# Reordered instruction sequences, a new order of the input loads, and filler matmuls in the head of a fused attention and gated-mixer kernel

## The chip, the cores and the metric

The kernel runs on one core of one Trainium2 chip. The metric is the device time of one execution in microseconds (us); several executions of each kernel are timed and the median is given. A profile of one execution shows every instruction of the engines: TensorE (PE: matmuls, PEld: its weight loads), VectorE (DVE), ScalarE (ACT), GpSimd (POOL) and SyncE (SP, which only issues transfers).

## The reference

One sequence of 2048 tokens with 448 features passes two residual blocks, all in bfloat16:

```python
# A: attention over a dilated local window of 8 positions, step 2, 16 heads of 28
qkv = layernorm(x) @ wqkv                       # 448 -> 3 x 448
logits = q[s] . k[s - 2*w] * 28**-0.5           # w = 0..7; positions before the start are masked
h = x + (softmax(logits) @ v[s - 2*w]) @ wo
# B: gated mixing over all tokens
z = gelu(layernorm(h) @ w_in)                   # 448 -> 1792
z1, z2 = z[..., :896], layernorm(z[..., 896:])
g = w_sp @ z2 + b_sp[:, None]                   # 2048 x 2048 over tokens
out = h + (z1 * g) @ w_out                      # 896 -> 448
```

## The kernel before, in words

Tokens lie in 16 blocks of 128. Unit u holds the blocks u and u+8, one in each half of the partitions (64 features of each, seven slices `c`), so that two matmuls of 64 rows run side by side. All of the work is cut into named tasks. Each engine runs its tasks strictly in the order that a table of names, `ORDER`, gives it; semaphore waits follow from reads and writes of buffers. A planner (`Planner.run`) walks the five lists together with assumed durations and transfer rates (`bw=`), and so settles which of the eight PSUM banks a task gets (`acq`, `rel`); most tasks take a pair of banks. The rates change no transfer, only this walk. `eng.alts` tasks run on the engine in whose list they stand: a PSUM copy `ev...` can be in ACT's list or in VectorE's.

The tasks, in the order of the data:

- `x0` to `x15`, `xhalo`, `wqk0`, `wqk1`, `wv0`, `wv1`: loads, issued by SP and ACT (line 577 and after). `c_...`: constants, among them `c_dup` on POOL, a matrix that doubles rows.
- `bn1_b` (two instructions, lines 683 and 684), `rs1_u` (the inverse root: on ACT for unit 0, on POOL otherwise), `nrm1_b` (line 699): LayerNorm of block b. `bnh`, `rsh`, `nrmh`, `tTh`, `evh`: the same for the 16 tokens before the second half.
- `tT1_u` (line 714) and `ev1_u`: transposes of unit u on TensorE and their copy to SBUF, for units 0 to 2. `tD1_u`, `tD2_u` (line 706): transposes by DMA for all others and for the second LayerNorm.
- `dpq`, `dpk` (line 778): the query and key weights are spread over the partitions by a matmul with `dup`; `rpq`, `rpk` (line 664) copy the result back, two slices each, padded from 28 to 32 columns a head.
- `mmq`, `mmk` (line 821), `mmv` (861): projections, the first two in three ranges of columns (128; 384 or 398; 512). `evq`, `evk`, `evv`: their copies.
- For each of nine tiles i of 114 tokens: `mml` (896, logits, four groups of 16 matmuls), `exp` (909), `mask` (916), `mmr` (925, row sums), `ln`, `rex` (the inverse of the sums), `mmo` (945, four groups of 16), `ot` (963).
- For each unit: `mmy` (999, output projection), `h`, a second LayerNorm `bn2`, `rs2`, `nrm2`, then `mmz2` (1019) and its gelu `ge` (for units 0 to 2 first a raw copy `zr`), `bn3`, `ag3`, `rs3`, `nrm3`.
- `mmz1` (1082) with gelu `gz1`; then the mixing `g` (1120, 448 matmuls of 512 columns), `ua`, `um`, the last projection `wo` (1153), `oa` and the store `st`.
- `wsp`, `bb`, `w_out`, `win`: the later weights; the `wsp` transposes are paced by waits on steps such as `ge4_1` (lines 1175 to 1190).

Before any data is there, `warm` (line 658) runs eleven matmuls on a constant tile. `tab` marks a load of ACT's function table for the first half; exp and gelu need different tables.

Of the kernel before, what the change touches and what calls it, by code (L numbers as in the profile page):

```python
# [40 lines left out]
        xhalo x1 x0 x11 x9 x2 wqk1 x3 x10 x14 x15 x6 x7 wv0 x12 x4 x13 tD1_3 x5 tD1_4 tD1_7 tD1_6 tD1_5 tD2_1 tD2_0  # L41
        wsp0_0 wsp0_8 tD2_3 tD2_2 tD2_4 wsp0_1 tD2_5 wsp0_2 wsp0_9 tD2_7 tD2_6 wsp0_10 bb wsp0_3 w_out wsp0_4 wsp0_11
        wsp1_8 wsp0_5 wsp1_0 wsp0_12 wsp1_9 wsp0_6 wsp0_13 wsp1_1 wsp0_7 wsp0_14 wsp1_2 wsp0_15 wsp1_3 wsp1_10 wsp1_4
        wsp1_11 wsp1_5 wsp1_12 wsp1_13 wsp1_14 wsp1_6 wsp1_15 wsp1_7 st7 st4 st5 st3 st8 st6 st0 st10 st9 st14 st13
        st2 st12 st12b st1 st15 st11
""",
    "pool": """
        c_mband c_V c_nhalf c_ident c_ones c_dup c_kpad rs1_3 rs1_1 rs1_2 rs1_4 rs1_7 rs1_6 rs1_5 c_wo0 rs2_0 rs2_1
        rs2_2 rs2_3 rs2_4 rs2_5 rs2_7 rs2_6 rs3_0 rs3_4 rs3_5 rs3_1 rs3_3 rs3_2 rs3_6 rs3_7
""",  # L50
    "dve": """
        c_warm c_wqp bnh c_eps c_wkp c_xpad bn1_8 bn1_1 nrmh bn1_0 evh bn1_11 nrm1_0 bn1_3 nrm1_8 bn1_9 bn1_2 nrm1_3
# [48 lines left out]
TU = 8.706  # L101
NE = 2
# [285 lines left out]
def bass_sequential_preLN__sliding_local_dilated__mixer_gmlp__prompt_kernel(  # L388
# [18 lines left out]
    with contextlib.ExitStack() as top:  # L407
# [826 lines left out]
```

## Time and profile before

| what | us |
|---|---|
| median of 4 runs | 256.08 |
| lowest and highest | 255.47 and 256.32 |
| profiled execution, its own time | 255.47 |
| its span, first to last instruction | 253.7 |
| PE, DVE, ACT busy | 243.9, 141.9, 93.4 |
| PE waits by the view of waits, all of them | 6.5 |
| first transpose `tT1_0`; first projection | 11.48; 13.42 |
| first mixing matmul `g` | 132.8 |

Times within the profile count from the start of the span. In a timeline row stand the start, the duration of the merged group, engine, line, operation, tiles and count; an idle stretch before it and what ended it stand in brackets. A row of the chain has start, duration, engine, output and line. A row of the waits has who waited, for whom, the total, how often, and the longest. The name `reg` in a row stands for several tiles that share a buffer.

### The profile page before, as it was taken

How to read it: one execution, taken by the hardware profiler on the slowest of the kernel's cores; microseconds unless marked ns; L12 is line 12 of the kernel's file. 1: busy time of each engine (PE TensorE's matmuls, PEld its weight loads, DVE VectorE, ACT ScalarE, POOL GpSimd, SP SyncE). 2: the span in 40 equal slices, each digit the busy share in tenths (PEclk: the TensorE clock that was granted, in tenths of full speed). 3: DMA queues.
4: the chain of work that ended last, by engine and by line, in shares of the span. 5: the costliest groups of instructions: out<-in, count | busy, mean ns of one | idle time of the engine just before them, and what ended most of it. 6: DMA issues, size and time to landing. Idle time of an engine off the chain costs nothing.

```text
span 253.7 us, 6518 instructions
## 1 busy us (share of the span) xinstructions
PE 243.9 (96%) x2924; PEld 123.8 (49%) x2924; DVE 141.9 (56%) x280; ACT 93.4 (37%) x109; POOL 28.9 (11%) x72
## 2 busy tenths in 40 slices
PE   6499999999999999999999999999999999999995
PEld 2285544546657545444444444444444444444453
DVE  6797547678688888995972003145107051370653
ACT  2688837257756785787485000000000000000000
POOL 6133300000202120311450000000000000000000
PEclk9889999999999999999999999999999999999999
DMA  6953403252063688799699992030000000010222
GB/s 223 264 96 68 89 16 75 50 129 58 6 96 64 118 149 144 155 179 236 115 193 156 184 185 40 3 83 0 0 3 0 0 18 18 3 36 0 72 71 78
DMA packets 55556, 22.03 MB, mean 87 GB/s; under 512 B 46936, under 2 KB 55400, under 8 KB 55528
## 3 DMA queue, kind: packets, MB, share of 16 engines
q1 hardware_dynamic: 52096, 16.79, 34.3%
q10 hardware_dynamic: 3432, 4.82, 8.0%
q8 instruction: 23, 0.38, 0.6%
q14 instruction: 5, 0.04, 0.1%
HBM read 8.39 MB, written 1.84 MB: 40 GB/s over the span
## 4 chain that ended last, share of the span: by engine, by line
PE 89%; DVE 3%; ACT 3%; DMA 2%; SPq 1%; issue 0%
PE psum L1120 38%; PE psum L821 10%; PE psum L1153 8%; PE psum L1019 8%; PE psum L1082 8%; PE psum L999 5%; PE psum L861 4%; PE psum L896 3%; PE psum L945 2%; DMA x_tm<-in_A_x_dram 2%; ACT reg L909 1%; DVE reg L916 1%; ACT xh L664 1%; DVE reg L963 1%; PE psum L925 1%; SPq L577 1%
## 5 line engine op out<-in xcount | busy, mean ns | idle before, releaser
L1130 DVE TENSOR_TENSOR ub<-psum,reg 128x512 bf16<-128x512 f32 x28 | 18.9, 686 | 67.4 <-PE psum L1120 67.2
L1120 PE MATMUL psum<-reg,z2p 128*128 128x512 bf16 x224 | 49.5, 379 | 0.0
L1120 PE MATMUL psum<-wspT_lo,z2p 128*128 128x512 bf16 x224 | 48.7, 379 | 0.0
L1120 PEld LDWEIGHTS psum<-wspT_lo,z2p 128*128 128x128 bf16 x224 | 21.8, 98 | 26.6 <-DVE z2p L1066 0.4
L1120 PEld LDWEIGHTS psum<-reg,z2p 128*128 128x128 bf16 x224 | 21.9, 98 | 26.2
L821 PE MATMUL psum<-xh,reg 64*128 64x128 bf16 (+3 forms) x336 | 27.4, 313 | 0.5 <-ACT xh L664 0.3
L1019 PE MATMUL psum<-w_in,xh 64*128 64x448 bf16 x224 | 22.9, 349 | 0.0
L664 ACT ACTIVATE reg<-psum 128x896 bf16<-128x896 f32 (+5 forms) x26 | 20.5, 829 | 4.6 <-PE psum L778 2.8
L1153 PE MATMUL psum<-reg 128*128 128x448 bf16 (+1 forms) x119 | 22.2, 341 | 0.0
L909 ACT ACTIVATE reg<-psum 128x928 bf16<-128x928 f32 x18 | 16.9, 943 | 14.3 <-PE psum L821 8.7
L1082 PE MATMUL psum<-xh,w_in 64*128 64x512 bf16 x196 | 22.1, 376 | 0.0
L683 DVE BATCH_NORM_STATS2 st<-x_tm 128x6 f32<-128x448 bf16 x32 | 19.4, 605 | 2.2 <-DMA x_tm<-in_A_x_dram 2.2
L1050 DVE BATCH_NORM_STATS2 st<-z2p 128x6 f32<-128x448 bf16 x32 | 17.6, 608 | 3.0 <-ACT z2p L1044 3.0
L821 PEld LDWEIGHTS psum<-xh,reg 64*128 64x128 bf16 x336 | 13.7, 98 | 9.9 <-ACT xh L664 1.2
L669 POOL TENSOR_SCALAR rs<-mv 128x2 f32<-128x2 f32 x23 | 6.3, 272 | 99.0 <-DVE mv L684 80.9
L670 POOL TENSOR_TENSOR rs<-rs,nhalf 128x2 f32<-128x2 f32 x23 | 16.7, 728 | 1.9
L1153 PEld LDWEIGHTS psum<-reg 128*128 128x128 bf16 x119 | 11.6, 98 | 9.9
L1162 DVE TENSOR_TENSOR tring<-psum,x_tm 128x448 bf16<-128x448 f32 (+1 forms) x17 | 9.8, 591 | 11.9 <-PE psum L1153 11.8
L666 DVE CAST reg<-psum 128x1024 bf16<-128x1024 f32 (+3 forms) x11 | 12.3, 1122 | 6.6 <-PE psum L821 6.6
L1019 PEld LDWEIGHTS psum<-w_in,xh 64*128 64x128 bf16 x224 | 10.9, 94 | 9.8 <-issue 0.4
L1092 ACT ACTIVATE reg<-psum 128x1024 bf16<-128x1024 f32 x14 | 13.9, 1025 | 3.5 <-PE psum L1082 3.5
L1082 PEld LDWEIGHTS psum<-xh,w_in 64*128 64x128 bf16 x196 | 9.5, 94 | 11.3
(66 smaller groups left out, 222.0 us busy)
## 6 DMA issues: line engine op xcount, KB each, us to landing
w_in<-in_B_w_in_dram ACTq DMA_DIRECT2D x4, 448.0 KB, 4.9
x_tm<-in_A_x_dram SPq DMA_DIRECT2D x15, 112.0 KB, 5.0
out_dram<-tring SPq DMA_DIRECT2D x15, 112.0 KB, 1.7
w_in<-in_B_w_in_dram ACTq DMA_DIRECT2D x4, 336.0 KB, 4.3
reg<-in_B_w_out_dram SPq DMA_DIRECT2D x1, 784.0 KB, 6.3
z2p<-in_A_wqkv_dram ACTq DMA_DIRECT2D x1, 672.0 KB, 4.9
reg<-in_B_b_sp_dram SPq DMA_DIRECT2D x1, 512.0 KB, 5.2
reg<-in_A_wqkv_dram ACTq DMA_DIRECT2D x1, 392.0 KB, 6.3
```

The source lines that it names most:

```text
L664: iss("act", lambda e: e.activation(dst, src, AF.Copy), reads=rd, writes=wr, after=after)
L670: iss("pool", lambda e: e.tensor_tensor(dst, dst, nh, ALU.pow), reads=rr + [r_nhalf], writes=rr)
L683: iss("dve", lambda e: e.bn_stats(st[:, b, :], x_tm[:, b, :]), reads=[r_x[b]], writes=[rl[b]])
L821: iss("pe", lambda e, c=c, s=s, gi=gi, lhs=lhs: e.matmul(psum[:, bk[s] * 512 + cw * gi:bk[s] * 512 + cw * gi + cw], lhs, xh[64 * s:64 * s ...
L909: iss("act", lambda e: e.activation(E[:, es[0], 2 * n:2 * n + 2, :], pair_view(lb, 0, 8 * JW), AF.Exp, scale=SCALE), reads=[r_bank[lb[0]], ...
L1019: iss("pe", lambda e, c=c, s=s: e.matmul(psum[:, zb[s] * 512:zb[s] * 512 + D], xh[64 * s:64 * s + 64, c, XO + 128 * u:XO + 128 * u + 128], ...
L1050: iss("dve", lambda e, b=b: e.bn_stats(st3[:, b, k, :], z2p[:, b, D * k:D * k + D]), reads=[r_z2[b][k]], writes=[r_st3[b][k]])
L1082: iss("pe", lambda e, c=c, s=s: e.matmul(psum[:, bk[s] * 512:bk[s] * 512 + 512], w_in[64 * s:64 * s + 64, c, 128 * f:128 * f + 128], xh[64 ...
L1092: iss("act", lambda e: e.activation(z1p[f].rearrange("p (s t) -> p s t", s=2)[:, :, 512 * ch:512 * ch + 512], pair_view(bk, 0, 512), AF.Ge ...
L1120: iss("pe", lambda e, b=b: e.matmul(psum[:, gb[0] * 512:gb[0] * 512 + 512], z2p[:, b, 128 * f:128 * f + 128], src[:, b, 512 * (tc % 2):512 ...
L1130: iss("dve", lambda e: e.tensor_tensor(ub[:, us_[0], :], psum[:, gb[0] * 512:gb[0] * 512 + 512], bb[:, 512 * tc:512 * tc + 512], ALU.add), ...
L1153: iss("pe", lambda e, f=f: e.matmul(psum[:, wb[0] * 512:wb[0] * 512 + c1 - c0], z1p[f][:, 128 * m:128 * m + 128], w_out[:, f, c0:c1], star ...
```

## The change

All five lists of `ORDER` are new; each holds the same tasks as before, except that ten PSUM copies change between ACT's and VectorE's list. Among other things SP's list begins with x0, xhalo and x3; POOL makes `dup` first; `ev1_0` moves to VectorE; ACT's `tab` moves from its end to its start; `mmz2_0_0` stands earlier. A new function `fill` issues matmuls of 512 columns on the constant tile `warm` into the bank that a task is about to use, ahead of four tasks of TensorE, five in all (`FILL`). The planner's assumed rates and issue times of some loads are others, and so is the step that its walk gives to the loads `win0`. Lines after the change are higher by some ten: 778 becomes 788, 714 becomes 722, 821 becomes 832, 896 becomes 908, 1019 becomes 1031, 1082 becomes 1094, 1120 becomes 1132.

```diff
 ORDER = {
     "sp": """
-        xhalo x1 x0 x11 x9 x2 wqk1 x3 x10 x14 x15 x6 x7 wv0 x12 x4 x13 tD1_3 x5 tD1_4 tD1_7 tD1_6 tD1_5 tD2_1 tD2_0
-        wsp0_0 wsp0_8 tD2_3 tD2_2 tD2_4 wsp0_1 tD2_5 wsp0_2 wsp0_9 tD2_7 tD2_6 wsp0_10 bb wsp0_3 w_out wsp0_4 wsp0_11
-        wsp1_8 wsp0_5 wsp1_0 wsp0_12 wsp1_9 wsp0_6 wsp0_13 wsp1_1 wsp0_7 wsp0_14 wsp1_2 wsp0_15 wsp1_3 wsp1_10 wsp1_4
...
+        x0 xhalo x3 x11 x9 x1 wqk1 x2 x12 x14 x10 x15 x6 x5 wv0 x13 x4 tD1_3 x7 tD1_6 tD1_5 tD1_7 tD1_4 tD2_0 tD2_1
+        tD2_2 wsp0_0 tD2_3 tD2_4 wsp0_8 wsp0_1 wsp0_9 wsp0_2 tD2_6 wsp0_10 wsp0_3 tD2_7 wsp0_11 tD2_5 wsp0_4 wsp0_12
+        w_out bb wsp0_13 wsp1_8 wsp0_5 wsp0_14 wsp1_0 wsp0_6 wsp1_9 wsp0_15 wsp1_1 wsp1_10 wsp0_7 wsp1_2 wsp1_11
...
     "pool": """
-        c_mband c_V c_nhalf c_ident c_ones c_dup c_kpad rs1_3 rs1_1 rs1_2 rs1_4 rs1_7 rs1_6 rs1_5 c_wo0 rs2_0 rs2_1
...
+        c_dup c_ones c_ident c_nhalf c_kpad c_V c_mband rs1_3 rs1_1 rs1_2 rs1_6 rs1_5 rs1_7 c_wo0 rs1_4 rs2_0 rs2_1
...
     "dve": """
-        c_warm c_wqp bnh c_eps c_wkp c_xpad bn1_8 bn1_1 nrmh bn1_0 evh bn1_11 nrm1_0 bn1_3 nrm1_8 bn1_9 bn1_2 nrm1_3
-        bn1_10 nrm1_1 nrm1_11 nrm1_9 nrm1_2 nrm1_10 bn1_4 bn1_7 bn1_12 bn1_6 bn1_15 bn1_14 nrm1_4 nrm1_12 nrm1_7
-        bn1_13 nrm1_6 nrm1_15 mask0 bn1_5 nrm1_14 evq1_3 nrm1_5 nrm1_13 evk1_1 ot0 evv1 mask1 evq2_2 evk2_0 evq2_0
-        mask2 evv3 ot1 evv4 evq2_1 evq2_3 mask3 ot2 h0 bn2_0 h1 mask4 bn2_9 bn2_8 ot3 bn2_1 mask5 nrm2_1 ot4 nrm2_9
-        nrm2_0 nrm2_8 evv7 h2 mask6 h3 ot5 bn2_2 bn2_3 bn2_11 bn2_10 mask7 ot6 h4 nrm2_3 nrm2_11 bn2_12 mask8 nrm2_2
-        bn2_4 nrm2_10 h5 nrm2_4 ot7 nrm2_12 bn2_13 bn2_5 h6 ot8 nrm2_5 bn3_0_0 h7 nrm2_13 bn2_7 bn2_15 bn2_6 bn2_14
-        nrm2_7 nrm2_15 nrm2_6 bn3_0_1 nrm2_14 ag3_0 bn3_2_1 bn3_3_1 bn3_4_1 nrm3_0 bn3_4_0 nrm3_8 bn3_3_0 ag3_4
...
+        c_warm c_eps c_wkp c_xpad c_wqp bnh bn1_8 bn1_0 nrmh bn1_3 nrm1_0 bn1_11 bn1_9 nrm1_8 evh bn1_1 ev1_0 bn1_2
+        bn1_10 nrm1_3 nrm1_1 nrm1_11 nrm1_9 nrm1_2 nrm1_10 bn1_14 bn1_6 bn1_13 bn1_15 nrm1_6 nrm1_14 bn1_5 bn1_7 mask0
+        nrm1_5 nrm1_7 nrm1_13 bn1_12 bn1_4 nrm1_15 evk1_2 nrm1_4 nrm1_12 evk1_1 ot0 evv1 evv3 mask1 evq2_0 mask2
+        evk2_0 ot1 evq2_2 mask3 ot2 evk2_3 h0 bn2_0 bn2_8 h1 mask4 ot3 bn2_1 bn2_9 mask5 ot4 evv5 nrm2_0 nrm2_8 nrm2_1
+        h3 nrm2_9 mask6 h2 ot5 bn2_10 bn2_3 bn2_11 bn2_2 mask7 h4 nrm2_3 nrm2_2 nrm2_10 ot6 nrm2_11 bn2_4 mask8 bn2_12
+        ot7 h5 nrm2_4 nrm2_12 bn2_13 ot8 h6 bn2_6 bn2_14 h7 bn2_5 bn2_7 nrm2_6 nrm2_14 nrm2_5 zr2_1 bn2_15 bn3_0_0
+        nrm2_7 nrm2_13 nrm2_15 bn3_1_0 bn3_4_0 bn3_4_1 bn3_0_1 bn3_1_1 bn3_2_0 bn3_2_1 bn3_3_1 bn3_3_0 bn3_5_0 ag3_3
...
     "act": """
-        x8 wqk0 rsh wv1 rpq1 rs1_0 rpk2 rpq0 rpq2 rpq3 ev1_0 rpk3 rpk0 rpk1 evq0_2 evq0_0 evk0_2 evk0_0 ev1_2 ev1_1
-        exp0_0 evv0 evk1_0 exp0_1 evq1_2 evq1_0 evq1_1 evk1_3 ln0 rex0 wo2 evv2 evk1_2 exp1_0 exp1_1 evk2_3 exp2_0 ln1
-        win1_00 exp2_1 wo1 wo3 rex1 wo0 ln2 exp3_0 win1_04 exp3_1 rex2 evk2_2 win1_10 evk2_1 ln3 exp4_1 win1_14 exp4_0
-        rex3 evv6 ln4 exp5_0 exp5_1 rex4 ln5 rex5 evv5 exp6_0 exp6_1 ln6 exp7_0 rex6 exp7_1 evv8 exp8_0 win0_00 zr0_1
-        exp8_1 ln7 zr1_1 win0_04 zr0_0 rex7 ln8 zr1_0 win0_10 rex8 ge0_1 ge0_0 ge3_0 win0_14 zr2_1 zr2_0 ge2_1 ge4_1
-        ge4_0 ge3_1 gz1_0_6 ge2_0 gz1_0_4 ge1_1 gz1_0_0 gz1_0_5 ge5_1 gz1_0_3 ge1_0 ge7_1 ge7_0 gz1_1_5 ge5_0 gz1_1_6
-        ge6_0 ge6_1 gz1_1_1 gz1_1_0 gz1_0_1 gz1_1_2 gz1_1_3 tab gz1_0_2 gz1_1_4
+        x8 wqk0 tab rsh wv1 rs1_0 rpq0 rpq1 rpq3 rpq2 rpk0 rpk1 rpk3 rpk2 evq0_0 evq0_2 evk0_2 evk0_0 ev1_1 ev1_2
+        exp0_0 evv2 exp0_1 evv0 evk1_0 evq1_1 evq1_2 evq1_0 ln0 rex0 evq1_3 win1_00 evk1_3 exp1_0 wo2 exp1_1 wo3
+        evk2_1 exp2_0 exp2_1 ln1 wo0 ln2 rex1 win1_04 exp3_0 evk2_2 wo1 exp3_1 evq2_1 rex2 ln3 win1_10 evq2_3 rex3
+        exp4_0 exp4_1 evv4 exp5_0 ln4 exp5_1 rex4 evv6 win1_14 exp6_0 ln5 exp6_1 win0_00 rex5 ln6 rex6 exp7_0 zr0_0
+        exp7_1 win0_04 evv7 ln7 exp8_0 evv8 exp8_1 rex7 zr1_0 win0_10 ln8 rex8 zr0_1 zr2_0 ge0_1 ge2_0 win0_14 zr1_1
+        ge1_0 ge4_1 ge0_0 ge3_1 ge4_0 ge2_1 ge3_0 gz1_0_6 gz1_0_1 ge1_1 gz1_0_4 gz1_0_2 ge6_1 gz1_0_3 ge7_0 ge5_0
+        ge5_1 gz1_0_0 gz1_1_0 ge7_1 ge6_0 gz1_1_2 gz1_0_5 gz1_1_3 gz1_1_6 gz1_1_5 gz1_1_4 gz1_1_1
 """,
     "pe": """
-        warm dpq1 tTh dpk2 dpk0 dpq2 dpq0 dpq3 tT1_0 dpk3 dpk1 mmq0_2 mmq0_0 mmk0_2 mmk0_0 tT1_2 tT1_1 mmv0 mml0_00
-        mml0_01 mmq1_1 mmk1_0 mml0_10 mml0_11 mmq1_2 mmq1_0 mmk1_3 mmq1_3 mmr0 mmv2 mmo0_0 mmo0_1 mmk1_2 mmo0_2 mmo0_3
-        mmk1_1 mmv1 mml1_00 mml1_01 mmq2_2 mml1_10 mml1_11 mmk2_3 mml2_00 mml2_01 mmk2_0 mmr1 mml2_10 mml2_11 mmq2_0
-        mmo1_0 mmv3 mmo1_1 mmo1_2 mmk2_2 mmr2 mmo1_3 mmv4 mml3_00 mml3_01 mmq2_1 mml3_10 mml3_11 mmq2_3 mmo2_0 mmo2_1
-        mmk2_1 mmo2_2 mmo2_3 mmy0 mml4_00 mml4_01 mmr3 mml4_10 mml4_11 mmy1 mmo3_0 mmo3_1 mmo3_2 mmv6 mmo3_3 mmr4
-        mml5_00 mml5_01 mml5_10 mml5_11 mmv5 mmo4_0 mmo4_1 mmo4_2 mmr5 mmo4_3 mmv7 mml6_00 mml6_01 mmy2 mml6_10
-        mml6_11 mmo5_0 mmo5_1 mmy3 mmo5_2 mmr6 mmo5_3 mml7_00 mml7_01 mmv8 mml7_10 mml7_11 mmy4 mmo6_0 mmo6_1 mmo6_2
-        mmo6_3 mml8_00 mml8_01 mmz2_0_1 mmr7 mml8_10 mml8_11 mmz2_1_1 mmz2_0_0 mmo7_0 mmo7_1 mmy5 mmo7_2 mmr8 mmo7_3
-        mmz2_1_0 mmz2_3_0 mmo8_0 mmo8_1 mmy6 mmo8_2 mmo8_3 mmz2_3_1 mmz2_2_1 mmy7 mmz2_2_0 mmz2_4_1 mmz2_4_0 mmz1_0_4
-        mmz1_0_6 mmz1_0_0 mmz1_0_5 mmz2_5_1 mmz2_5_0 mmz1_0_3 mmz2_7_1 mmz1_1_5 mmz2_7_0 mmz1_1_6 mmz2_6_0 mmz1_0_1
-        mmz1_1_2 mmz2_6_1 mmz1_1_1 mmz1_1_0 mmz1_1_4 mmz1_1_3 mmz1_0_2 g0_2_0 g0_0_0 g0_1_0 g0_0_1 g0_2_1 g0_1_1
...
+        warm dpq0 dpq1 tTh dpq2 dpq3 dpk1 dpk0 tT1_0 dpk2 dpk3 mmq0_0 mmq0_2 mmk0_2 mmk0_0 tT1_1 mml0_00 mml0_01 tT1_2
+        mmv0 mmv2 mml0_10 mml0_11 mmq1_1 mmk1_0 mmq1_2 mmq1_0 mmr0 mmk1_2 mmq1_3 mmo0_0 mmo0_1 mmk1_1 mmo0_2 mmo0_3
+        mmk1_3 mmv3 mml1_00 mml1_01 mmv1 mml1_10 mml1_11 mmk2_1 mml2_00 mml2_01 mmq2_0 mml2_10 mml2_11 mmr1 mmk2_0
+        mmo1_0 mmr2 mmo1_1 mmo1_2 mmk2_2 mmo1_3 mml3_00 mml3_01 mmq2_2 mml3_10 mml3_11 mmq2_1 mmo2_0 mmo2_1 mmq2_3
+        mmo2_2 mmr3 mmo2_3 mmk2_3 mmo3_0 mmo3_1 mmy0 mmo3_2 mmo3_3 mml4_00 mml4_01 mmy1 mml4_10 mml4_11 mmv4 mml5_00
+        mml5_01 mml5_10 mmr4 mml5_11 mmv6 mmo4_0 mmo4_1 mmo4_2 mmo4_3 mmv5 mmr5 mml6_00 mml6_01 mmy3 mml6_10 mml6_11
+        mmo5_0 mmo5_1 mmy2 mmo5_2 mmo5_3 mmr6 mmv7 mml7_00 mml7_01 mmz2_0_0 mml7_10 mml7_11 mmo6_0 mmo6_1 mmy4 mmo6_2
+        mmo6_3 mmr7 mml8_00 mml8_01 mmv8 mml8_10 mml8_11 mmz2_1_0 mmo7_0 mmo7_1 mmy5 mmo7_2 mmr8 mmo7_3 mmz2_0_1
+        mmo8_0 mmo8_1 mmy6 mmo8_2 mmo8_3 mmz2_2_0 mmz2_1_1 mmy7 mmz2_2_1 mmz2_4_1 mmz2_3_0 mmz2_3_1 mmz2_4_0 mmz1_0_2
+        mmz1_0_6 mmz1_0_1 mmz1_0_4 mmz1_0_0 mmz2_6_1 mmz1_0_3 mmz2_7_0 mmz2_5_0 mmz2_6_0 mmz2_5_1 mmz1_1_0 mmz2_7_1
+        mmz1_1_2 mmz1_1_1 mmz1_0_5 mmz1_1_4 mmz1_1_3 mmz1_1_6 mmz1_1_5 g0_2_0 g0_2_1 g0_1_0 g0_2_2 g0_0_0 g0_0_1
+        g0_0_2 g0_0_3 g0_2_3 g0_1_1 g0_1_2 g0_1_3 g0_0_4 g0_1_4 g0_1_5 g1_6_0 g0_0_5 g0_4_0 g1_1_0 g0_1_6 g1_0_0
...
+FILL = {"dpk1": 2, "tT1_0": 1, "dpk3": 1, "mmk0_2": 1}
...
         def ld_x(b, prio, eng="sp"):
             t_x[b] = dma(eng, "x%d" % b, lambda e: e.dma_start(x_tm[:, b, :], X[128 * b:128 * b + 128, :]),
-                         128 * D * 2, prio=prio, writes=[r_x[b]], bw=250.0)
+                         128 * D * 2, prio=prio, writes=[r_x[b]], bw=330.0, issue=0.5)
...
-                D * D * 2, prio=prio, writes=[r_wv[s]], bw=240.0)
+                D * D * 2, prio=prio, writes=[r_wv[s]], bw=230.0)
...
         t_w["qk", 0] = dma("act", "wqk0", lambda e: e.dma_start(
-            384 * 2 * D * 2, prio=-11.0, writes=[r_wqk[0]], bw=300.0)
+            384 * 2 * D * 2, prio=-11.0, writes=[r_wqk[0]], bw=380.0)
...
+        def fill(name, bank):
+
+            for _ in range(FILL.get(name, 0)):
+                iss("pe", lambda e: e.matmul(psum[:, bank * 512:bank * 512 + 512], warm[:, 0:128], warm[:, :]),
+                    reads=[r_warm], writes=[r_bank[bank]])
...
             def em_t():
+                fill("tT%d_%d" % (which, u), bk[0])
                 o = bk[0] * 1024
                 for c in range(NC7):
...
-                def em(j=j, bk=bk, hs=hs, c0=c0):
+                def em(j=j, bk=bk, hs=hs, c0=c0, p=p):
+                    fill("dp%s%d" % (p, j), bk[0])
                     for h in hs:
                         iss("pe", lambda e, h=h: e.matmul(psum[:, bk[h] * 512:bk[h] * 512 + D], dup[64 * h:64 * h + 64, :],
...
+                    def em(t0=t0, cw=cw, isq=isq, g0=g0, bk=bk, ng=ng, off=off, p=p, rx=rx, ch=ch):
+                        fill("mm%s%d_%d" % (p, ch, g0), bk[0])
                         for gi in range(ng):
...
-        chain(t_win[1] + t_win[0], [t_xh[NU - 1]] * 4 + [by["exp8_0"]] * 4, False)
+        chain(t_win[1] + t_win[0], [t_xh[NU - 1]] * 4 + [by["exp6_0"], by["exp7_0"], by["mask7"], by["exp8_0"]], False)
```

## The prediction

> **What bounds the kernel now.** I read the windows view first, then the chain of waits, then TensorE's waits, then its timeline. The columns of the windows view are: stretch and its length, busy time of PE, PEld, DVE, ACT and POOL, granted clock, DMA share, GB/s.
>
> ```profile
> 4.50:8.00 3.50, 2.74 (x22) 0.94 (x20) 2.85 (x10) 1.33 (x4) 1.32 (x6) 1.00 1.10 324
> 8.00:11.40 3.40, 0.35 (x1) 0.09 (x1) 1.69 (x6) 2.83 (x4) 0.22 (x1) 1.00 1.12 291
> 11.40:14.80 3.40, 3.17 (x38) 2.18 (x40) 3.30 (x11) 2.35 (x4) 2.24 (x5) 0.50 0.75 148
> 14.80:17.30 2.50, 2.50 (x91) 2.40 (x88) 2.47 (x7) 2.01 (x4) 0.34 (x1) 1.00 0.67 59
> 55.00:100.00 45.00, 44.11 (x1032) 27.07 (x1031) 36.58 (x58) 31.15 (x35) 6.44 (x12) 1.00 0.54 92
> 100.00:132.80 32.80, 32.80 (x321) 15.39 (x318) 27.73 (x71) 23.76 (x27) 10.04 (x20) 1.00 0.85 168
> 132.80:253.70 120.90, 118.04 (x569) 55.33 (x567) 39.34 (x79) 4.14 (x4) 0.00 (x0) 1.00 0.25 50
> ```
>
> From 100 us to the last matmul TensorE never idles. A spatial block `g` (16 matmuls of 512 columns) takes 3.45 us, 216 ns each, and each row of that stretch repeats to 1 ns. So all that follows about 100 us has a fixed length: whatever the work before it gains or loses reaches the end one for one, and nothing after it can give time back. The head is the loose part: almost no matmuls in 8 to 11.4 us, then half the clock for 3.4 us.
>
> ```profile
> PE psum L714 <- DVE tring L699: 2.2, 1, 2.2
> PE psum L778 <- ACT reg L664: 1.0, 1, 1.0
> ```
> ```profile
> 4.21 5.96 DMA x_tm<-in_A_x_dram
> 10.19 0.64 DVE st L683
> 10.85 0.18 DVE mv L684
> 11.03 0.40 DVE tring L699
> 11.48 0.94 PE psum L714 x7
> 12.45 0.93 ACT xh L664
> 13.42 3.93 PE psum L821 x112
> ```
>
> The chain names the head's cause. Block x3 is issued as SP's eighth load at 4.21 and lands at 10.17. VectorE runs in order, and `bn1_3` (L683 at 10.19) stands ahead of `nrm1_8` (L699 at 10.95). `nrm1_8` needs nothing of x3, but the transposes `tT1_0` (L714) need it. They start at 11.48, ACT's copy `ev1_0` ends at 13.37, and the 112 matmuls of `mmq0/mmk0` (L821) run from 13.42 to 17.29.
>
> The stretch from 17 to 100 is nearly full, but it is not at TensorE's rate where short matmuls stand together:
>
> ```profile
> 22.65 0.44 PE L896 MATMUL psum<-reg 32*64 32x58 bf16 x32
> 59.63 0.95 PE L945 MATMUL psum<-reg 64*32 64x58 bf16 x48
> 62.46 2.09 PE L896 MATMUL psum<-reg 32*64 32x58 bf16 x64
> 67.59 0.39 PE L925 MATMUL psum<-reg,ones 64*32 64x464 bf16 x8 [0.45 <-DVE reg L916]
> ```
>
> Two groups of 16 cost about 0.4 us, four cost four to five times that: after some 32 short ones each further group takes up to 0.63 us (39 ns a matmul).
>
> **What the Trainium skill says.** "TensorE: Matmul & The Clock Gate", Part 1: the array's clock falls to half after an idle window of about 3.4 us and returns after a busy one; the window is free-running. The trace agrees: half clock from 11.37 to 14.78, 3.41 us, after the empty window before it; the window 4.5 to 8, 2.74 us busy, did not trigger it. "DMA: Bandwidth & Descriptors", Issuing engines are not separate DMA queues: loads of SP and ACT share the same 16 DMA engines and interleave. It agrees: x3 waited behind `wv1`, which ACT issued at 3.66 and which landed at 9.96. "VectorE: DVE Perf Modes", perf-mode tier table: a copy out of PSUM runs at up to twice the base rate. No row before shows a wide bf16 one.
>
> **The change, part by part.**
>
> *Loads and LayerNorm order.* x0 and x3 become SP's first and third loads. The bytes ahead of `wqk0` hardly change, so it lands about 6.2 again, and x3 takes the place of the load issued third, which landed at 6.36. x11 and x9 stay at 6.6 and 6.9. VectorE then runs `bn1_3` at 6.4, `nrm1_0`, `bn1_11`, `bn1_9`, `nrm1_8`: from the pitches of the timeline (0.73 a `bn`, 0.42 to 0.5 a `nrm`) `nrm1_8` ends at 6.4+0.73+0.42+0.73+0.73+0.47 = 9.4. `tT1_0` starts at 9.5 instead of 11.48. Now `evh`, `bn1_1` and then `ev1_0` run on VectorE: `bn1_1` to 10.15, `ev1_0` 0.55 to 1.05 us (the float copy of 896 columns takes 1.07, half of it by the skill's page). I take 1.0: it ends at 11.15. `mmq0_0` starts at 11.2.
>
> *What is late next.* ACT's chain of weight copies: six of 896 columns at a pitch of 0.82 and two of 448 at 0.45 to 0.5, from 6.64 (as now): 6.64+4.9+1.0 = 12.55. Without `ev1_0` in it, this ends 2.9 us before today's 15.4. `mmq0` needs its first half only; two blocks of 0.78 us bring 12.75, one filler 13.0, and the last copy (12.55) is there. `mmk0` ends at 13.0+1.56 = 14.55, against 17.29: 2.7 us. `mml0_00` waits for the copy `evk0_0` until about 15.35 after `tT1_1`: 0.35 lost. `tT1_2`, `mmv0`, `mmv2` (now early), `mml0_1x` follow, and `mmq1_1` starts at 19.55. Before it started at 20.23 without `mmv2` (1.45) and `mml0_1x` (0.38) done. Head: 0.68+1.45+0.38 = **2.5 us**. `tD1_3`, whose source `nrm1_11` ends about 13.8, should land at 13.85+3.82 = 17.7, in time. POOL makes `dup` first instead of last; `wqk0` hides that.
>
> *Fillers.* Five matmuls of 512: 5 x 0.216 = 1.1 us, 2.1 at half clock. Four stand where TensorE waits for a copy or for `nrm1_8`, so cost nothing; the fifth (before `mmk0_2`) is counted above. They take 7.96 to 11.37 from one projection pair to about 2.0 us of matmuls. Is that enough for the clock? The trace brackets the threshold between 0.35 and 2.74. I take yes. With no, the 3.4 us from 11.4 run at half: up to 1.7 us of work lost, so 1.5 of the 2.5 gone. If a filler waits on a bank, it adds 0.2.
>
> *The attention stage.* Counting runs of short groups before: they take 23.1 us in all, of which about 1.7 are waits and pairs behind a drained queue. Priced by the trace (pair 0.30 or 0.39, three 0.88, four 1.44, longer 1.7) the new order sums to 20.8, plus five pairs close behind a `mmv` that itself follows short ones (0.26 each): 22.1. New tight spots: `mmr2` comes 2.2 us after the last logit group of its tile, while exp 0.94 + mask 1.12 + hand-overs need 2.5; `mmr4` has 2.3. With others of that size 0.8. Net gain **0.2**, bounds -0.8 to +1.5.
>
> *z1, z2, spatial.* The same blocks at the same durations: 0. Their covers: `tD2_5` is last, behind `nrm2_15`, about 105 to 108 us; `mmz2_5_0` comes about 112. `win0_14` issues about 92.5 and took 6.3 us before; the first `mmz1` comes about 101. `wsp0_7` and `wsp0_15` are queued behind `wsp1_9`, which waits for `ge6_0` (about 121.5): at 1.34 us a transpose and 4 us to land, 131; `g1_6_0` reads its last blocks about 139. If one of these covers is gone, TensorE waits in place.
>
> *Table load.* The reload at 132.4 (two loads of 1.28 us) moves to the start; TensorE does not wait for ACT there: 0. Of the tail, `oa11` 0.62 and a store, 2.8 us, is as before.
>
> **Sum.** The profiled execution took 255.47 (span 253.7 plus 1.77 around it), 0.61 under the median of the runs, 256.08. 255.47 - 2.5 - 0.2 = 252.8; at the same distance to the median 253.4.
>
> **Rivals.**
> (a) *The clock still drops.* For: 2.0 us of 3.4 is less than any window that is seen to hold it, and a free-running window can fall badly. Against: it is six times the window that lost it. 253.4 + 1.5 = 254.9.
> (b) *The head's gain turns into waits of the attention stage*, whose exp, mask and row-sum chain follows its own pace: before, `mmr5` waited 0.45 for a mask. Against: only 1.1 us of such waits show from 17 to 100, with ACT and VectorE 69 and 81% busy. 256.1.
> (c) *Slower.* `bn3_0_0` stands ahead of `nrm2_7/13/15` on VectorE; it waits for `ge0_0`, which ACT does after a table load and after `ge4_1`. If `ge0_0` comes late, `tD2_7`, `wsp0_11`, `tD2_5` and the pacing of all spatial weights shift, and TensorE stops at `mmz2_7_0/5_0`. It decides once `tD2_5` lands over 4 us late (about 112); slower in total from 7 us late. `tD2_4` has shown 6.8 us from issue to landing among other loads. At 8.5 us late: 257.4.
> (d) *The filler does nothing by itself*: the reordered head leaves no window idle anyway. Same time as forecast.
>
> **How the numbers follow.** Main case, (d) within it: 0.66, 253.4, own range 252.3 to 254.5. (a) 0.18, 254.9, mostly still faster. (b) 0.09, about no change. (c) 0.07. About 0.3% (0.77 us) is what a measurement of this kernel can tell from no change. Faster: 0.66 + 0.15 = 0.81; same: 0.03 + 0.09 = 0.12; slower 0.07. The range reaches from the short copy plus the upper bound of the attention stage (252.0) over (a) to 255.5.
>
> **What would show it.** In the profile after: `tT1_0` at about 9.5, L832 (the projections) starting near 11.2 with one block of four ended by 12.0; no stretch at clock 0.50 after 8 us; `mmq1_1` near 19.5; the first `g` near 130.1; after that the same 3.45 us a block. A half-clock window from 11.4 would show (a); a head as forecast with the first `g` at 132.8 (b); waits of L1031 or L1094 (z2, z1) on a DMA (c). A head gain under 1 us would make the prediction wrong.

## The result, and the profile after

The changed kernel takes 255.31 us (median; 254.50 to 256.11), the kernel before 256.02 in the same comparison: a ratio of 0.9973, interval 0.9964 to 0.9982. It is faster by 0.7 us, where 2.7 were forecast. The profiled execution took 256.81 (span 255.1), 1.5 over its own median, so its gaps are read below for their place, and what they are worth is taken from the runs.

First the windows view, in the stretches that were shown of before, and rows of the timeline, of the head and of the first `g`.

```profile
4.50:8.00 3.50, 2.87 (x19) 0.95 (x17) 3.39 (x9) 2.49 (x6) 1.51 (x8) 1.00 0.97 293
8.00:11.40 3.40, 3.20 (x41) 1.67 (x43) 3.28 (x10) 3.40 (x6) 1.88 (x4) 1.00 1.10 273
11.40:14.80 3.40, 3.40 (x104) 2.96 (x99) 3.03 (x9) 2.66 (x5) 0.93 (x2) 1.00 0.96 173
...
55.00:100.00 45.00, 41.68 (x1000) 23.97 (x1000) 35.54 (x58) 28.80 (x32) 6.47 (x12) 0.96 0.51 87
100.00:132.80 32.80, 32.80 (x326) 15.57 (x321) 28.47 (x72) 22.36 (x25) 9.43 (x19) 1.00 1.05 186
```
```profile
9.42 0.55 PE L722 MATMUL psum<-ident,tring 128*128 128x128 bf16 x7
10.12 0.59 DVE L673 COPY xh<-psum 128x896 bf16<-128x896 bf16 x1
10.77 1.78 PE L832 MATMUL psum<-xh,reg 64*128 64x128 bf16 x56
...
19.93 1.31 PE L832 MATMUL psum<-xh,reg 64*128 64x384 bf16 x14
134.19 6.00 PE L1132 MATMUL psum<-wspT_lo,z2p 128*128 128x512 bf16 x27
```

The same row before:

```profile
132.77 9.46 PE L1120 MATMUL psum<-wspT_lo,z2p 128*128 128x512 bf16 x43
```

The head did what was forecast: the hole from 8 to 11.4 is filled, the half clock behind it is gone, `tT1_0` starts at 9.42, the projections (L832) at 10.77. The first mixing block `g` starts at 134.19 nevertheless, against 132.77 before. All that was won, and more in this execution, went between 20 and 100 us, where TensorE is busy 41.68 of 45 us instead of 44.11. Its waits as summed from 17 us on come to 5.0 us, against 1.0 before. First the sums before, then the sums after, then the rows with an idle time in brackets that name the places:

```profile
PE psum L925 <- DVE reg L916: 0.6, 2, 0.5
PE psum L896 <- DVE reg L666: 0.2, 1, 0.2
PE psum L821 <- ACT xh L664: 0.2, 1, 0.2
```
```profile
PE psum L937 <- DVE reg L928: 1.3, 2, 0.8
PE psum L957 <- ACT z2p L671: 1.2, 1, 1.2
PE psum L873 <- issue: 0.9, 1, 0.9
PE psum L1011 <- DVE reg L975: 0.8, 2, 0.5
PE psum L832 <- DMA xh<-tring: 0.6, 1, 0.6
PE psum L873 <- ACT reg L921: 0.2, 1, 0.2
```
```profile
35.07 1.86 PE L832 MATMUL psum<-xh,reg 64*128 64x512 bf16 x14 [0.60 <-DMA xh<-tring]
42.33 0.39 PE L937 MATMUL psum<-reg,ones 64*32 64x464 bf16 x8 [0.81 <-DVE reg L928]
62.09 0.39 PE L937 MATMUL psum<-reg,ones 64*32 64x464 bf16 x8 [0.45 <-DVE reg L928]
62.98 2.42 PE L873 MATMUL psum<-reg,xh 64*64 64x448 bf16 x28 [0.25 <-ACT reg L921]
79.49 0.31 PE L957 MATMUL psum<-reg 64*32 64x58 bf16 x32 [1.17 <-ACT z2p L671]
84.86 0.77 PE L873 MATMUL psum<-reg,xh 64*64 64x448 bf16 x12 [0.86 <-issue]
```

These are, in order, `mmk2_1` for a transposed load, `mmr2` and `mmr4` for the mask, `mmv6` for exp, `mmo6_0`, and a gap in the middle of `mmv8` ("issue": the profile shows nothing that it waits for). The load that `mmk2_1` waits for is `tD1_4`, SP's last of the first five: issued at 28.22, landed at 34.98, 6.8 us. On ScalarE's queue `win1_00` (448 KB) had been issued at 27.52; before, it was issued at 40.80, when all five had landed.

### The profile page after: what moved, and what is told of

It reads as the page before. It is cut to its first block, busy times and chain, and to the rows that moved or that the text cites. A ratio compares the mean times of both kernels' runs of the same rounds, so it can differ in the third digit from the quotient of the medians.

```text
span 255.1 us, 6525 instructions
## 1 busy us (share of the span) xinstructions
PE 244.2 (96%) x2929; PEld 122.2 (48%) x2929; DVE 142.2 (56%) x280; ACT 91.9 (36%) x107; POOL 29.5 (12%) x72
## 4 chain that ended last, share of the span: by engine, by line
PE 87%; DVE 4%; DMA 4%; ACT 3%; issue 1%; SPq 0%
PE psum L1132 38%; PE psum L1165 8%; PE psum L1094 8%; PE psum L1031 8%; PE psum L832 8%; PE psum L1011 4%; PE psum L873 4%; PE psum L908 3%; DMA xh<-tring 3%; PE psum L957 2%; ACT reg L921 1%; PE psum L937 1%; DVE reg L975 1%; DMA xhalo<-in_A_x_dram 1%; DVE reg L928 1%; ACT reg L671 1%
## 5 line engine op out<-in xcount | busy, mean ns | idle before, releaser
L832 PE MATMUL psum<-xh,reg 64*128 64x128 bf16 (+3 forms) x336 | 27.1, 306 | 0.6 <-DMA xh<-tring 0.6
L671 ACT ACTIVATE reg<-psum 128x896 bf16<-128x896 f32 (+5 forms) x28 | 22.4, 839 | 5.8 <-PE psum L832 3.5
L676 POOL TENSOR_SCALAR rs<-mv 128x2 f32<-128x2 f32 x23 | 6.9, 300 | 100.4 <-DVE mv L691 80.8
L832 PEld LDWEIGHTS psum<-xh,reg 64*128 64x128 bf16 x336 | 13.4, 94 | 9.7 <-issue 1.1
L873 PE MATMUL psum<-reg,xh 64*64 64x448 bf16 x252 | 14.8, 370 | 1.2 <-issue 0.9
L1174 DVE TENSOR_TENSOR tring<-psum,x_tm 128x448 bf16<-128x448 f32 (+1 forms) x17 | 9.7, 591 | 11.2 <-PE psum L1165 11.2
L975 DVE TENSOR_TENSOR reg<-psum,reg 128x912 bf16<-128x912 f32 x9 | 11.1, 1233 | 7.7 <-PE psum L908 2.1
```

The costliest lines, as they stand in the source:

```text
L671: iss("act", lambda e: e.activation(dst, src, AF.Copy), reads=rd, writes=wr, after=after)
L832: iss("pe", lambda e, c=c, s=s, gi=gi, lhs=lhs: e.matmul(psum[:, bk[s] * 512 + cw * gi:bk[s] * 512 + cw * gi + cw], lhs, xh[64 * s:64 * s ...
L873: iss("pe", lambda e, c=c, s=s, w=w: e.matmul(psum[64 * w:64 * w + 64, bk[s] * 512:bk[s] * 512 + D], xh[64 * s:64 * s + 64, c, XO - HALO + ...
```

## The experiments

The runs of before in these comparisons had medians from 255.88 to 256.18; every ratio is against the runs beside it. Before again, unchanged, shows the noise.

> The kernel before, unchanged, profiled once more and timed, to see the granted clock of several executions. If the half-clock window of 3.4 us belongs to the idle head, it shows in nearly every execution (clock 0.993) at about 8 to 15 us, wherever the free-running window falls. If it is a matter of chance, about half of the executions show a clock of 1.00 and are about 1 us shorter. Ratio to before 1.000.

It gave 255.96, ratio 0.9993 (0.9980 to 1.0007). All that lies within 0.2% of 1 is no difference. None of its 22 executions kept the full clock: 14 have a mean of 0.987, which is two windows of 3.4 us at half, and 8 have 0.993, which is one. So the half clock comes with this kernel every time and is not a matter of chance.

In all the runs that follow, only the lists and `FILL` are edited in the changed kernel, so they all have its assumed rates and its step for `win0`, the one in the order of before too.

**The change without its five fillers.**

```diff
-FILL = {"dpk1": 2, "tT1_0": 1, "dpk3": 1, "mmk0_2": 1}
+FILL = {}
```

> The changed kernel without the five fillers, all else the same. If the fillers hold the clock in the head: a half-clock window near 11 us, the projections of the first range up to 1.5 us longer, about 256.3 (ratio to before 1.001). If the reordered head leaves no idle window by itself: the same time as with fillers, 255.3 (0.997), or 0.2 us less.

256.06, ratio 1.0004 (0.9980 to 1.0027). In its profile the clock is half from 10.50 to 13.91; 8 of its 14 executions lost at least one window. Beside the change's 0.9973 the fillers are worth some 0.8 us here, though the two intervals touch.

**The new head with the order of before behind it.** Each engine's list follows the change up to the end of the second projection range, and from there the sequence of before.

```diff
 SP    ... tD1_7 tD1_4
-tD2_0 tD2_1 tD2_2 wsp0_0
+tD2_1 tD2_0 wsp0_0 wsp0_8
 ScalarE  ... rex0 evq1_3
-win1_00 evk1_3 exp1_0 wo2
+evk1_3 wo2 exp1_0 exp1_1
 TensorE  ... mmo0_3 mmk1_3
-mmv3 mml1_00 mml1_01 mmv1
+mmv1 mml1_00 mml1_01 mmq2_2
```

> The new lists and fillers up to the end of the second range of the projections (mmk1_3), the old order for all that follows. If the head's gain of about 2 us is real and the new order of the attention stage loses it again: 254.0 (ratio 0.992), the first g near 130.7. If the head's gain is swallowed by the pace of the attention stage whatever its order: 255.3 to 256 (0.997 to 1.000).

253.91 us against 256.13 beside it, ratio 0.9930 (0.9912 to 0.9947): 1.8 us by the ratio, 2.2 by the medians, and faster than both kernels. Its first `g` is at 131.35, 1.4 us earlier than before. So the head's gain does reach the end when the order behind it lets it.

**The head of before (no fillers), with the new order behind it.**

```diff
 TensorE  ... mmo0_3 mmk1_1
-mmv1 mml1_00 mml1_01 mmq2_2
+mmv3 mml1_00 mml1_01 mmv1
-FILL = {"dpk1": 2, "tT1_0": 1, "dpk3": 1, "mmk0_2": 1}
+FILL = {}
```

> The old lists up to the end of the second range of the projections (mmk1_1), no fillers, the new order for all that follows. If the new order of the attention stage loses by itself: 257 to 257.5 (ratio 1.004 to 1.006). If it is neutral and only follows the head: 256 (1.000).

257.73, ratio 1.0071 (1.0048 to 1.0095): slower than before by 1.8 us by the ratio, 1.6 by the medians. The two halves of the change pull in opposite directions. The new head with fillers is worth 0.7% on the old rest and (1.0071 to 0.9973) 1.0% on the new one; the new rest costs 0.7% behind the old head and (0.9930 to 0.9973) 0.4% behind the new one, 1.1 to 1.8 us.

**The weight load `win1_00` later.** The first of four tests of named waits; each starts from the changed kernel.

```diff
 ScalarE
-rex0 evq1_3 win1_00 evk1_3 exp1_0 wo2 exp1_1 wo3 evk2_1 exp2_0 exp2_1 ln1 wo0
+rex0 evq1_3 evk1_3 exp1_0 wo2 exp1_1 wo3 evk2_1 exp2_0 exp2_1 ln1 win1_00 wo0
```

> One move in the changed kernel: ScalarE issues win1_00 (448 KB) after ln1, as before, instead of after evq1_3. Theory W (the 1.6 us that the new attention order costs are the waits that the profile after names, and TensorE gets back what is taken away): tD1_5 lands about 3 us after its issue instead of 6.8, the wait of mmk2_1 for it (0.60) goes, 255.3 - 0.6 = 254.7. Theory P (the waits are symptoms: exp, mask and row sums follow their own pace, and TensorE only waits for the next of them instead): within 0.2 of 255.3.

254.39, ratio 0.9941 (0.9921 to 0.9962): 0.8 to 0.9 us faster than the change, for the place of one issue. The load concerned is `tD1_4` (the text above names `tD1_5`, which is another): it now lands at 32.62, 4.4 us after its issue, and TensorE's waits no longer list it.

```profile
PE psum L937 <- DVE reg L928: 1.3, 2, 0.8
PE psum L1011 <- DVE reg L975: 0.8, 2, 0.5
PE psum L957 <- ACT reg L921: 0.4, 1, 0.4
PE psum L873 <- ACT reg L921: 0.2, 1, 0.2
```

The gap inside `mmv8` is gone too, and `mmo6_0` waits 0.42 instead of 1.17, so this run alone does not prove that the late `tD1_4` is the whole of it. The converse run is cleaner.

**The same load earlier, in the kernel with the new head and the old rest.**

```diff
 ScalarE
-evq1_3 evk1_3 wo2 exp1_0 exp1_1 evk2_3 exp2_0 ln1 win1_00
+evq1_3 win1_00 evk1_3 wo2 exp1_0 exp1_1 evk2_3 exp2_0 ln1
```

> The converse of the run with w_in later: the kernel with the new head and the old rest (253.9), with one move, win1_00 issued by ScalarE after evq1_3, as in the change, ahead of tD1_4. Theory L (the 448 KB ahead of one transposed load are the largest single part of what the attention order costs): tD1_4 lands 2 to 3 us later, mmk1_1's or mmk2's wait for it grows by 0.6 to 1.0, 254.6 to 254.9. Theory N (in the changed kernel the move's worth was a chain of accidents after it): within 0.3 of 253.9.

256.94 (254.40 to 261.25), ratio 1.0033 (1.0012 to 1.0053): 2.6 us slower than without the move by the ratios, 3.0 by the medians, more than any theory gave. Part of it is the clock: 10 of the 22 executions have a mean clock of 0.993 or less, none of the 6 without the move has. The 12 others have a median of 256.3, which is 2.4 us slower. TensorE's row, first with the load late, then early:

```profile
32.90 1.69 PE L832 MATMUL psum<-xh,reg 64*128 64x512 bf16 x14 [0.43 <-DMA xh<-tring]
```
```profile
35.45 1.69 PE L832 MATMUL psum<-xh,reg 64*128 64x512 bf16 x14 [2.59 <-DMA xh<-tring]
```

`tD1_4` lands 6.8 us after its issue, as in the change, but this order asks for it at 32.86 (35.45 less 2.59), 1.6 us earlier than the change does. This profile kept the full clock. The first `g` moves from 131.35 to 134.21, 2.9 us, of which 2.55 are there already after this wait: it reaches the end whole. Within the change the same lateness showed as only 0.60, because `mmk2_1` stands later.

**Row sums later.** `mmr2` and `mmr4` each get one block more between their tile's last logits and themselves, which gives exp and mask time.

```diff
 TensorE
-mmo1_0 mmr2 mmo1_1 mmo1_2 mmk2_2 mmo1_3
+mmo1_0 mmo1_1 mmo1_2 mmk2_2 mmr2 mmo1_3
-mml5_10 mmr4 mml5_11 mmv6
+mml5_10 mml5_11 mmv6 mmr4
```

> Two moves in the changed kernel, on TensorE: mmr2 goes behind mmk2_2 (as before), mmr4 behind mmv6, so that each has a projection or value block more between its tile's last logits and itself. W: the two waits for the mask (0.81 and 0.45) shrink to under 0.3 together, 255.3 - 1.0 = 254.3. P: the mask chain is the bound, the wait reappears at the next row sum or output group; within 0.2 of 255.3.

255.58, ratio 0.9987 (0.9974 to 1.0001): no gain, though both waits of 1.26 us in all left the trace. As `tD1_4`'s lateness might have hidden it, the same two moves were made with `win1_00` late:

```diff
 ScalarE
-rex0 evq1_3 win1_00
+exp2_1 ln1 win1_00
 TensorE
-mmo1_0 mmr2 mmo1_1 mmo1_2 mmk2_2 mmo1_3
+mmo1_0 mmo1_1 mmo1_2 mmk2_2 mmr2 mmo1_3
-mml5_10 mmr4 mml5_11 mmv6
+mml5_10 mml5_11 mmv6 mmr4
```

> The changed kernel with w_in later (254.4) and with the two row-sum moves (alone 255.6, no gain). If the row sums' waits are on a chain that has its own pace, nothing more: 254.3 to 254.8. If the late tD1_4 had hidden their gain: 253.4 to 253.9.

254.77, ratio 0.9959 (0.9945 to 0.9974), against 254.39 without them. Then one move at a time, since one could gain what the other loses:

```diff
 TensorE (win1_00 late as above)
-mml5_10 mmr4 mml5_11 mmv6
+mml5_10 mml5_11 mmv6 mmr4
```

> The changed kernel with w_in later (254.4), and of the two row-sum moves the second alone: mmr4 behind mmv6. In the trace of the run with both moves TensorE is 0.97 us later than without them ahead of mmr4's place and only 0.10 later at mmv6, so this move should give back 0.9 in the profile (its wait of 0.45, mmv6's of 0.25), and take away the half clock that some runs have after the window around 60 us: 253.7 to 254.0. If tile 4's chain only waits elsewhere then: 254.3 to 254.6.

```diff
 TensorE (win1_00 late as above)
-mmo1_0 mmr2 mmo1_1 mmo1_2 mmk2_2 mmo1_3
+mmo1_0 mmo1_1 mmo1_2 mmk2_2 mmr2 mmo1_3
```

> The changed kernel with w_in later (254.4), and the first move alone: mmr2 behind mmk2_2. In the trace of the run with both, its own wait of 0.81 is gone, but the next two groups wait 0.25 and 0.51 for what follows from the later row sum (its reciprocal, the normalised output copy). If so, nothing or a loss: 254.4 to 254.9. If the wait of 0.81 comes back in time: 253.6.

254.50 (0.9934; 0.9910 to 0.9957) and 254.75 (0.9949; 0.9933 to 0.9965). Neither differs measurably from 254.39. Where the time goes can be seen in TensorE's rows, first with `mmr2` later, then with `mmr4` later:

```profile
44.87 1.68 PE L832 MATMUL psum<-xh,reg 64*128 64x512 bf16 x14 [0.25 <-ACT reg L945]
47.06 0.46 PE L908 MATMUL psum<-reg 32*64 32x58 bf16 x32 [0.51 <-DVE reg L975]
```
```profile
63.25 1.83 PE L957 MATMUL psum<-reg 64*32 64x58 bf16 x64
...
66.78 0.39 PE L937 MATMUL psum<-reg,ones 64*32 64x464 bf16 x8 [0.25 <-DVE reg L928]
...
67.92 1.69 PE L1011 MATMUL psum<-reg 128*128 128x448 bf16 x8 [0.17 <-DVE reg L975]
```

The late `mmr2` makes `ln`, the reciprocal and `ot` late in turn: the next projection waits 0.25 behind ScalarE's `ln` (L945) and the logits 0.51 for the bank that `ot` (L975) frees, 0.76 in place of 0.81. The late `mmr4` is followed by waits of 0.25 and 0.17, and the four output groups behind it take 1.83 instead of some 1.5. The waits for the mask are one view of a chain (exp, mask, row sum, reciprocal, output copy) with a pace of its own.

**`mmz2_0_0` later**, with its copy `zr0_0`, both near where they were before.

```diff
 TensorE
-mml7_01 mmz2_0_0 mml7_10 mml7_11
+mml7_01 mml7_10 mml7_11
-mml8_10 mml8_11
+mml8_10 mml8_11 mmz2_0_0
 ScalarE
-exp7_0 zr0_0 exp7_1 win0_04 evv7 ln7 exp8_0 evv8 exp8_1
+exp7_0 exp7_1 win0_04 evv7 ln7 exp8_0 evv8 exp8_1 zr0_0
```

> mmz2_0_0 moves on TensorE from ahead of mml7_10 to behind mml8_11, and its eviction zr0_0 on ScalarE from behind exp7_0 to behind exp8_1 (both near where they were before). W: the 1.17 us that mmo6_0 waits for the bank that zr0_0 frees go, 255.3 - 1.1 = 254.2. P: mmo6_0 then waits for exp or mask of its own tile, within 0.3 of 255.3.

257.03, ratio 1.0041 (1.0022 to 1.0060): a loss of 1.7 us. Both theories missed. Its rows:

```profile
75.63 1.59 PE L908 MATMUL psum<-reg 32*64 32x58 bf16 x64
77.16 0.55 PE L957 MATMUL psum<-reg 64*32 64x58 bf16 x14
78.44 0.26 PE L957 MATMUL psum<-reg 64*32 64x58 bf16 x18 [0.74 <-issue]
78.63 2.98 PE L1011 MATMUL psum<-reg 128*128 128x448 bf16 x8
```

With `mmz2_0_0` between them the four logit groups had taken 0.50 and 0.46; in one run they take 1.59. The last row runs at half clock (1.69 elsewhere): the window of short matmuls ahead of it lost the clock. And the idle time is still there with `zr0_0` out of the way, now 14 matmuls into a run of 32, where the profile shows nothing that is waited for. So the bank of `zr0_0`, to which the profile put the 1.17 us, was not its cause. The 14 matmuls of `mmz2_0_0` no longer stand ahead of the gap, and the gap has moved 14 matmuls down the list: it keeps its place in the count of TensorE's instructions (see the last section).

**All three moves together.**

```diff
 ScalarE
-evq1_3 win1_00 evk1_3
-exp7_0 zr0_0 exp7_1
+exp2_1 ln1 win1_00
+exp8_0 evv8 exp8_1 zr0_0
 TensorE
-mmo1_0 mmr2 mmo1_1
-mml5_10 mmr4 mml5_11
-mml7_01 mmz2_0_0 mml7_10
+mmk2_2 mmr2 mmo1_3
+mmv6 mmr4 mmo4_0
+mml8_11 mmz2_0_0 mmz2_1_0
```

> The moves of the three runs before together. W: the named waits were 0.6 + 1.26 + 1.17 = 3.0 us, more than the 1.6 that the order costs, so some comes back as other waits; 253.0 to 253.8, at or below the kernel with the new head and the old rest (253.9). P: 255 or more. In between: the rest lies in how the short matmuls stand together, and shows in no wait.

255.73, ratio 1.0019 (0.9997 to 1.0042): about what the gain of one (0.9), the loss of another (1.7) and nothing from the third add up to.

**The fillers alone**, in the order of before.

```diff
 ORDER as before
+FILL = {"dpk1": 2, "tT1_0": 1, "dpk3": 1, "mmk0_2": 1}
```

> The instruction order of before, in whole, with the five filler matmuls added at the same four places (no reordered loads, no moved copy). Theory H (the reordering of the head makes the gain in time, the filler only keeps the half clock away): tT1_0 still waits for x3 until 11.4, the fillers run before it, and the window 8 to 11.4 gets some more work; if the clock holds, the 3.4 us at half clock return up to 1.0, minus up to 0.5 for fillers on the path: 255.2 to 255.7. Theory F (the filler makes the gain): 254.5 or less. If the half-clock window stays, 256.0 to 256.5.

257.04, ratio 1.0041 (1.0024 to 1.0058): 1.1 us slower, worse than any theory gave. The clock still drops, only later, on the projections:

```profile
9.13:12.55 3.42, 1.80 (x13) 0.75 (x12) 2.53 (x7) 2.37 (x4) 1.37 (x4) 1.00 1.13 265
12.55:15.96 3.41, 3.41 (x56) 2.84 (x56) 3.38 (x10) 2.83 (x5) 1.44 (x3) 0.50 0.46 107
```

1.8 us of matmuls in a window did not hold the clock, and the half clock now lies wholly on matmuls: the first 56 projections take 3.03 us instead of the change's 1.78. 13 of its 22 executions have a mean clock of 0.987, two such windows.

**The new head on the old rest, without fillers.**

```diff
-FILL = {"dpk1": 2, "tT1_0": 1, "dpk3": 1, "mmk0_2": 1}
+FILL = {}
```

> The kernel with the new head and the old rest (253.9), without the five filler matmuls. H: where the clock holds by itself 0.2 less than 253.9, where it drops at 10.5 us (as in the changed kernel without fillers) 0.9 more: median 254.3 to 254.8. F: 255.5 or more.

254.07, ratio 0.9918 (0.9892 to 0.9944), against 0.9930 with them: no difference that can be told. Its profile has half the clock from 9.34 to 12.75. Three of its six executions lost such a window (median 254.4), and the three others have a median of 253.2; with the fillers all six kept the clock and have 253.9. So the fillers do keep the clock there, but they cost about what they save.

## Why the prediction was right or wrong

**The head: right in mechanism, 0.4 us short.** Forecast and measured: `tT1_0` 9.5 and 9.42; `ev1_0` 1.0 and 0.59 (the lower bound was the right one); `mmq0_0` 11.2 and 10.77; end of `mmk0` 14.55 and 14.54 (the earlier start went into projections of 1.78 and 1.74 us a pair instead of 1.56); `mml0_00` 15.35 and 15.59 behind `evk0_0`; `tD1_3` landing at 17.7 and 17.45; `mmq1_1` 19.55 and 19.93. The head's gain by the same sum is 20.23 + 1.83 - 19.93 = 2.1, against 2.5. The runs agree: 1.8 to 2.2 us for the new head on the old rest. (The prediction's sum to the end of `nrm1_8` comes to 9.48, not 9.4; its 9.5 for `tT1_0` holds.)

**The fillers: the conclusion held in this kernel, its reason didn't.** There was no half clock after 8 us, so rival (a) failed at its place. But it took the busy time for what decides, and about 2.0 us for enough: a window of 1.80 us dropped the clock in the run with the fillers alone and one of 2.58 in the run without them, while one of 2.24 kept it (last section). Here the reordered work and the fillers together kept 3.39 of 3.42 us busy (8.83 to 12.25). That is more than the 2.0 forecast. Case (d), that the filler does nothing by itself, fits the time of the kernel with the old rest, but not its reason: without fillers half of the executions there lose the clock. In the change the filler was worth some 0.8 us.

**The attention stage: this is the step that failed.** Forecast was a net gain of 0.2 with bounds of -0.8 and +1.5; the runs show a loss of 1.1 to 1.8, outside these bounds. The short groups were not at fault: counted like the prediction's 23.1 us, those of the change take 20.1 without waits in the profiled execution, where 22.1 were forecast. What failed is the term for new waits, 0.8 us: with the waits they take 24.3, and all waits from 17 us on are 5.0 in that execution against 1.0 before. The sum counted the two row sums, which are found at 0.81 and 0.45 (0.3 and 0.2 were implied) and proved to be worth nothing when moved. It left out the transfers that the new order moves. `win1_00` goes 13 us forward, past the issue of `tD1_4`; the prediction followed `tD1_3`, `tD2_5`, `win0_14` and `wsp`, and not this one. Putting it back returned 0.8 to 0.9 us. The rest of the loss, 0.5 us between the kernel with `win1_00` late (254.39) and the one with the whole old rest (253.91), is not in the row sums, and not in the place of `mmz2_0_0`. `win1_00` is not the whole of the 1.8 behind the old head either: there it is issued at 31.37, behind `tD1_5`, and nothing waits for it. What that profile does have, as the change's has, are two gaps near 80 and 85 us, here of 1.09 and 0.69. With the old order of the stage no profile has them. The last section reads them as late instructions. How much of the loss in the medians they make was not measured, so the rest stays open. The stage also lost a clock window in some executions (below), which no step had counted.

**Rivals.** (b), the head's gain turns into waits of the attention stage, is the nearest: about no change was its time. Its reason, the pace of exp, mask and row sum, is real in the trace, but the new head on the old rest shows that the stage can pass on some 2 us of gain; it was the new order that gave the gain away, and not the pace. (c) did not occur: nothing waits in `mmz2_5_0`, `mmz2_7_0`, `mmz1` or `g`, and from 100 us on the blocks have the lengths of before. Nothing on TensorE waits for the table load, as said. (The 1.1 us of waits "from 17 to 100" in (b) are 1.0, and the shares of 69 and 81% are those of 55 to 100 us.)

## What to carry to other kernels

When a list is reordered, follow every transfer on every queue to its new neighbours before pricing the matmuls: one load of 448 KB, issued 0.7 us ahead of a transposed load that is needed soon, cost 0.8 us in one kernel and 2.6 or more in another. If a gap has no visible cause, count instructions: a gap that stays at the same count while tasks move past it does not belong to a task. A wait in a trace is worth what returns when its cause is gone, and inside a chain with its own pace (the row sums here) that was nothing. Change the head and the steady part of a kernel in separate steps: here the better half alone gave about 2 us and both together 0.7.

## What the runs showed of the hardware

- **The clock window judges more than busy time.** The Trainium skill ("TensorE: Matmul & The Clock Gate", Part 1) has a free-running window of 3413 ns that watches how busy the array is; the records here change in steps of 3.41 us, at a different phase in each execution. The busy time in the profile does not order the windows: 1.80 (9.13 to 12.55 of the fillers alone), 1.89 (5.92 to 9.34 of the new head on the old rest without fillers) and 2.58 us (7.09 to 10.50 of the change without fillers) lost the clock, while 2.24 (4.26 to 7.67 of before, run again) and 2.61 (5.42 to 8.83 of the change) kept it. In the change a window in mid-kernel lost it, 2.71 us busy, all of it matmuls of 32 and 64 rows:

```profile
60.04:63.45 3.41, 2.71 (x96) 1.79 (x92) 2.54 (x3) 3.22 (x4) 0.00 (x0) 1.00 0.02 5
63.45:66.86 3.41, 3.41 (x92) 2.11 (x86) 2.23 (x5) 2.93 (x4) 1.83 (x2) 0.50 0.00 0
```

  18 of 44 executions of the change have a mean clock of about 0.993, one such window, and a median of 255.78; the others have 254.98, so it costs 0.8 us where it occurs. With `mmr4` moved, which ends the waits of 0.45 and 0.25 near 62, none of 45 executions in three kernels had a clock under 0.998. With `mmr2` alone 6 of 22 had. With all three moves 10 of 22 had: there the profile shows another window lost, 76.2 to 79.6 us, as with `mmz2_0_0` alone.
- **A transposed load takes longer beside a plain load.** The skill ("DMA: Bandwidth & Descriptors", Queues, rings and completion order) says that each engine takes turns between queues by packets. The trace fits. From 27 to 36 us, with packets, MB and their share of the 16 DMA engines' time, SP's queue of transposes (q1) and ScalarE's (q10) moved:

```profile
q1 hardware_dynamic: 1959, 0.48, 35.1%
q10 hardware_dynamic: 398, 0.56, 28.2%
```

  That is 245 against 1400 bytes a packet. That the profile's packets are those of the skill's page is taken, not shown. `tD1_4` took 6.8 us in it, 4.4 without `win1_00`.
- **TensorE stands still at a fixed count of its instructions.** Count the weight loads, matmuls and waits of TensorE in the trace, in order of time. Eight profiles have a gap near 78 us before instruction 3265 or 3266, whatever task stands there (1.17 us in the change, 0.29 in the smallest), and three of them another just 256 later. Without the fillers there are 10 instructions fewer ahead, and both gaps of the change sit five matmuls further on, in `mmo6_0` after 5 and in `mmv8` after 21 instead of 16:

```profile
78.14 0.21 PE L957 MATMUL psum<-reg 64*32 64x58 bf16 x5
79.47 0.30 PE L957 MATMUL psum<-reg 64*32 64x58 bf16 x27 [1.12 <-issue]
...
83.01 1.32 PE L873 MATMUL psum<-reg,xh 64*64 64x448 bf16 x21
84.57 0.57 PE L873 MATMUL psum<-reg,xh 64*64 64x448 bf16 x7 [0.24 <-issue]
```

  In every profile the queue that the profile calls instruction (q8) brought 23 packets of 16 KB, one for each 256 of TensorE's 5900 instructions or so. Each of the eight gaps near 78 ends 1.25 to 1.53 us after the end of such a packet. In the six kernels with the old order of this stage that packet begins 0.5 to 1.6 us after TensorE's instruction 3010, 256 ahead, and there is no gap; in the two with the new order and no gap, 2.1 us after; in the eight with a gap, 2.2 to 3.6. So the plain reading is that TensorE waited for its next block of instructions, and that the gaps which the profile puts down to `zr0_0` or to exp at this count are of the same kind. Why the packet is late was not tried. ScalarE's queue issues `win0_00` (448 KB) at 72.04 in the change, just ahead of it, and at 83.71 before.
- A copy of 128x896 bfloat16 from PSUM to SBUF takes VectorE 0.59 us, against 1.07 to 1.08 on average for one from float. The skill's table ("VectorE: DVE Perf Modes", the perf-mode tier table) caps a copy out of PSUM at twice the base rate, which fits.
